# Token sums joined, gates of three batches loaded at once, and a weight quarter moved between value blocks, in a fused attention and expert-mixture kernel

## The chip, the cores and the metric

The kernel runs on one core of one Trainium2 chip. The metric is the device time of one execution in microseconds (us). A core has a tensor engine (PE, with PEld for its weight loads), a vector engine (VectorE, DVE in the profile), a scalar engine (ScalarE, ACT), GpSimd (POOL) and a queue engine (SyncE, SP). Each works through its own instructions in the order in which the program gives them, and waits on semaphores for the others. Transfers are issued by POOL (software queue) and by SP and ACT (hardware queue) and share 16 DMA engines.

## The reference, cut to what matters

Attention over 4 batches, 8 heads, 768 tokens and head size 64, in which a query sees 4 sink tokens and the last 128 tokens; its output, as 3072 rows of 512, goes through a mixture of 4 experts.

```python
keep = is_sink | ((rel >= 0) & (rel < 128))
a = softmax(where(keep, q @ k.T / 8, -1e9))
x = (a @ v).transpose(0, 2, 1, 3).reshape(3072, 512)
p = domain_probs / (domain_probs.sum(-1, keepdims=True) + 1e-09)
for e in range(4):
    out += p[:, e:e + 1] * (relu(x @ w1[e]) @ w2[e])     # w1[e]: 512x1024, w2[e]: 1024x512
```

## The kernel before, in words

**Tiling.** A batch has three groups of 256 tokens. For a group and a pair of heads, attention makes scores (`scores`, L704), exponentials on ScalarE (L729), a mask product on VectorE (L723, in batch 0 L738), and values (`values`, L763 for the sinks and L770 for the rest); reciprocals (L797) and a product (L800, or L815 on ScalarE) give `onat`, which is turned into `xT`: in batch 0 by PE (`turn`, L834, copied out at L286), later by a DMA transpose on SP (L787). In `values` the first index of `od` behind the partitions is the half of the group's 256 tokens, so `xT[b, g][:, 0]` holds the first 128 tokens and `xT[b, g][:, 1]` the second.

**The mixture.** A unit is a group and an expert. Its first product, with w1, is plain for the units that come before `START` (L1114) and else a seven-product scheme in place of eight (L1204; for the last 20 units with tokens on the partitions, L1316). The scheme needs four sums of token blocks for each group, made in `tokens` (L1170) into a tile `T`, and sums of the weight blocks: `weight_form1` (L390 to L396, tiles `vf`) and `weight_form` for w2 (L357 to L363, tiles `wf`). A unit's result, gated and clipped, lies in `H`. The second product is plain for the first two groups of batch 0 (L1575, evacuated by VectorE at L1585 and L1587 from two PSUM tiles, `acc` 0 and 1, in turn) and the seven-product scheme after that (L1489, with sums of blocks of `H` at L1430 and L1407).

**Gates.** Most units multiply by a row of gates, broadcast to all partitions by DMA (`load_gate`, L475). The 20 units with tokens on the partitions ("turning" units) use `own_gates`, which holds the probabilities by token; `own_load` (L1613) loads it, `own_made` (L1616) divides it by its sums with four VectorE operations (L1618 to L1621). `OWN = 2` says that it begins with batch 2, and `TURNED_UNITS = (4, 0)` that the turning units are all but the first four from there. A turning unit's result is made in a half-buffer (`rest`, or a resting gate tile) and brought into its `H` by a DMA transpose on SP (L1297).

**H buffers.** `NH = 6` tiles `H` in a pool, and three more in the freed `qkT` once attention is over (`widened`). A unit takes its `H` when it opens (`opened`), turning units too.

**The order of the work.** The kernel's own planner writes out the order of every engine's instructions. It keeps a clock for each engine in `t`, a cost for each kind of operation (`pe`, `act`, `dve`, `pool`, `sp`), and puts evacuations and sums into `pend` with a ready time and a slack; `flush` takes them in turn. The loop from L1660 picks the next PE step among attention, first products, second products. `idle_products` (L577, L580) writes PE products without use where the planner sees a gap in the first 20 us. `SOON` is the planner's time from which weight sums may be written while batch 0's attention is still going on (L1708); `SHARE_OF` sets how fast attention of the next batch advances beside the mixture.

**The first loads.** POOL issues two value blocks `vx`, four blocks of q and k, two more value blocks, and then the four quarters of w1 of expert 0 (L505 to L513). Between them it makes `sel2` (L522) and the batch's sink values `vsd` (L643).

Of the kernel before, what the change touches and what calls it, by code (L numbers as in the profile page):

```python
# [16 lines left out]
def kernel(  # L17
# [44 lines left out]
    OWN = 2  # L62
    TURNED_UNITS = (4, 0)
# [4 lines left out]
    SHARE_OF = (1.01, 0.92, 0.96)  # L68
# [18 lines left out]
    SCALED = 300  # L87
    SHARED = 2
# [4 lines left out]
    SOON = 34000  # L93
    NEARLY = 2
    ROWED = 24000
    GATED = 38000
    W2AT = 2
# [411 lines left out]
    load_v(0, (2, 3))  # L509
    load_w1(0, 4, [0])  # L510
    load_w1(0, 4, [1])
# [235 lines left out]
    def values(b, hp, g):  # L747
# [6 lines left out]
        for qi in range(2):  # L754
            qb = 2 * g + qi
            terms = []
            c = 0
            for (kb, q0, nq) in GROUPS[g]:
                if q0 <= qb < q0 + nq:
                    terms.append((kb, c + (qb - q0) * P))  # L760
                c += nq * P
            if g > 0:
                nc.tensor.matmul(  # L763
                    od[:, qi], lhsT=sinkA[b][:, (qb - 2) * P:(qb - 1) * P], rhs=vsd[b][:, hp],
                    start=True, stop=False, skip_group_check=True,
                )
                cols += 2 * DX
            for ph in range(2):
                for i, (kb, c) in enumerate(terms):
                    nc.tensor.matmul(  # L770
                        od[:, qi, ph], lhsT=a[:, ph, c:c + P], rhs=vx[kb][:, 2 * hp + ph, 0:DX],
                        start=(g == 0 and i == 0), stop=(i == len(terms) - 1), skip_group_check=True,
                    )
                    cols += DX + 5
# [174 lines left out]
    NH = 6  # L949
# [6 lines left out]
    class Mixture:  # L956


        def __init__(self):
# [14 lines left out]
            self.turning = set(mine[TURNED_UNITS[0]:len(mine) - TURNED_UNITS[1]])  # L974
            self.gated = [u for u in self.order if u not in self.turning]
# [9 lines left out]
            self.stored, self.homed = [], False  # L985
            self.spare, self.lent = [], {}
# [7 lines left out]
        def room(self):  # L994
            if self.units and self.units[0] in self.turning and self.halves() < 2:
                return False
            return self.spare or self.live < NH

# [13 lines left out]
        def widened(self):  # L1012

            x = sb.tile([P, 2, NHP, S], BF16, name="qkT", tag="qkT", bufs=1)
            x = x.rearrange("p i h n -> p (i h n)")
            n = 2 * QF * 2 * P
            self.spare = [x[:, i * n:(i + 1) * n].rearrange("p (k f t n) -> p k f t n", k=2, f=QF, t=2) for i in range(3)]
            self.rest("onat", 2, 2, t["pe"])
            self.rest("aT", 4, 1, t["pe"])

        def opened(self, b, g, e):

            if self.spare:
                self.H[b, g, e] = self.spare.pop()
                self.lent[b, g, e] = self.H[b, g, e]
            else:
                self.H[b, g, e] = mo.tile([P, 2, QF, 2, P], BF16, name="H", tag="H", bufs=NH)
                self.live += 1
            fast = self.is_fast(b, g, e)
            if (b, g, e) in self.turning:  # L1030
                self.G[b, g, e] = [self.half(), self.half()]

            def complete(at):
                self.H_at[b, g, e] = at
                self.finished.add((b, g, e))
                if (b, g) >= PAIRS[0]:
                    self.waiting.append((b, g, e))
                    load_gates()
                    if not TURNED_UNITS[1] and self.gated[-1] == (b, g, e):
                        self.rest_gates()  # L1040

# [19 lines left out]
        def firsts(self):  # L1061
# [15 lines left out]
            if n < WIDE and self.units and (self.units[0][0] or loaded) and early <= MIX and self.room() and not (early + zero and self.live >= NH - 1):  # L1077
                yield self.unit_ready(*self.units[0], QF), (OPEN if n else 2) - EARLY, ("unit",)
# [67 lines left out]
        def tokens(self):  # L1146
# [13 lines left out]
            B11, B21, B12, B22 = x[:, 1, 0:2], x[:, 1, 2:4], x[:, 0, 0:2], x[:, 0, 2:4]  # L1160
# [5 lines left out]
            self.T[b, g] = {"P1": B11, "P2": B21, "P3": B22, "P4": T[:, 3], "P5": T[:, 0], "P6": T[:, 1], "P7": T[:, 2]}  # L1166
            steps = [(T[:, 0], B12, B11), (T[:, 1], B22, T[:, 0]), (T[:, 2], B22, B12), (T[:, 3], B21, T[:, 1])]

            def run(engine):
                nc.vector.tensor_sub(*steps.pop(0))  # L1170
                done = dve(G, rate=1.92)
# [109 lines left out]
        def emit_turning(self, u, m, ready):  # L1281
            b, g, e = u["unit"]
            H, X, at = self.H[b, g, e], self.G[b, g, e], u["at"]
            n = QF * P
            assert len(own_steps) == 4
            if m in ("P1", "P5"):
                spare = [i for i in range(6) if ring[i] <= ready + 40]
                spare.sort(key=lambda i: (whole[i], ring[i]))
                if m == "P1":
# [5 lines left out]
                    def turned(k):  # L1295
                        def turn(at):
                            nc.sync.dma_start(  # L1297
                                out=H[:, k].rearrange("c f t n -> c (f t) n"), in_=X[k].rearrange("p f t n -> p (f t n)"), transpose=True,
                            )
                            done = sp(at, issue=1330, takes=1400, turning=True) + LANDS  # L1300
                            self.H_part[b, g, e](done)
                            self.H_part[b, g, e](done)
                            self.resting.append((done, X[k]))
# [83 lines left out]
        def chore(self):  # L1387
# [12 lines left out]
            if self.last:  # L1400
                b, g, e = u = self.last[0]
                if (b, g, "P2") not in self.products:
                    self.last.pop(0)

                    def form(engine):
                        H12 = self.H[b, g, e][:, 1, :, 0]
                        nc.vector.tensor_sub(H12, H12, self.S[b, g][1][:, e])  # L1407
                        self.S4_at[u] = dve(QF * P, rate=1.92)
                    return go(form, self.until(b, g, e, "P3"))
# [9 lines left out]
            self.waiting.pop(0)  # L1419
            if (b, g) not in self.S:  # L1420
                self.S[b, g] = [mo.tile([P, E, QF, P], BF16, name=f"S{i}", tag=f"wide{i}", bufs=1) for i in range(2)]
            H = self.H[b, g, e]
            H11, H21, H22 = H[:, 0, :, 0], H[:, 0, :, 1], H[:, 1, :, 1]
            S = self.S[b, g]
            steps = [(nc.vector.tensor_add, S[0][:, e], H21, H22), (nc.vector.tensor_sub, S[1][:, e], S[0][:, e], H11),
                     (nc.vector.tensor_sub, H21, H11, H21)]

            def form(engine):
                x = steps.pop(0)
                x[0](*x[1:])  # L1430
                at = dve(QF * P, self.stored[-1] if (b, g) == PAIRS[0] else 0.0, rate=1.92)
                if steps:
                    go(form, self.until(b, g, e, "P6 P7".split()[len(steps) == 2]))
                else:
                    self.S_at[u] = at
                    self.last.append(u)
            return go(form, self.until(b, g, e, "P6"))
# [5 lines left out]
        def operand(self, b, g, e, m):  # L1443
            H = self.H[b, g, e]
            if m in ("P5", "P6"):
                return self.S[b, g]["P5 P6".split().index(m)][:, e]
# [23 lines left out]
        def emit_product(self):  # L1470
# [30 lines left out]
            if m == CHAIN[-1]:  # L1501
                if (b, g, e) in self.lent:
                    self.spare.append(self.lent.pop((b, g, e)))
                else:
                    self.live -= 1
# [56 lines left out]
        def emit_second(self):  # L1562
# [35 lines left out]
            if s == 1:  # L1598
                self.live -= 1
# [16 lines left out]
    def own_made():  # L1616
# [13 lines left out]
        later("dve", t["pe"], 5000, run)  # L1630
# [29 lines left out]
    while mix.more() or att.more():  # L1660
# [14 lines left out]
        if rowed == 1 and now > GATED:  # L1675
            rowed = 2
            load_gates()
        if not att.more() and not loaded:
            loaded = 1
            turns += [(1, tb) for tb in range(NQB)]  # L1680
            loads.append((load_w1, 3))
            for tb in range(NQB):
                if tb == W2AT:
# [26 lines left out]
        if ahead + 1 < B and not att.more() and (ahead == 0 or (ahead + 1, 0) in turned_at) and (ahead == 0 or mix.done >= sum(work[:ahead]) * LEAD[ahead - 1]):  # L1710
            ahead += 1
            if ahead == 1:
                own_load()
            elif ahead == 2:
                own_made()
# [14 lines left out]
        opts.append((max(p, now), HIGH_PRODUCT if behind > BEHIND or mix.live >= FULL or wide and TURN_ABOUT and mix.turn_about else LOW_PRODUCT, "product", None))  # L1730
# [65 lines left out]
```

## Time and profile before

| | |
|---|---|
| median of 3 runs | 354.03 us (353.99 to 354.43) |
| the profiled execution's own time | 354.08 us |
| its span, first to last instruction | 352.4 us |
| granted PE clock | 1.00 |
| busy share PE, PEld, DVE, ACT, POOL | 98%, 76%, 81%, 59%, 21% |
| DMA | 45.61 MB, mean 129 GB/s |

All times inside the execution count from the span's start. "Busy" counts instructions that work; a matmul's end is modelled, so a busy PE need not be at its peak. A row such as `15.70 0.39 PE L580 ... x2` reads: from 15.70 us, for 0.39 us, on PE, line 580, two instructions; in brackets at its end stands idle time before it and what ended that. The chain of waits is the path back from the last instruction, at each step to what released it.

### The profile page before, as it was taken

The page shows a single profiled execution, that of the slowest core. Times are in us where ns is not written, and L with a number is a line of the kernel's source. Part 1 is how long each engine was busy: PE and PEld are TensorE (multiplying, and loading weights), DVE is VectorE, ACT ScalarE, POOL GpSimd, SP SyncE. Part 2 cuts the span into 40 slices and gives each one's busy share as a digit, 9 for nine tenths or more (in the row PEclk, how much of TensorE's full clock was granted, in tenths as well). Part 3 has the DMA queues.
Part 4 walks back from the last instruction along what each step waited for, and adds up shares of the span by engine and source line. Part 5 has one row for each costly group of instructions (what it writes and reads, how often), then busy time and mean ns, then how long its engine had stood idle before and what let it go on. Part 6 is the DMA issues. An engine that isn't in the chain of part 4 may idle for free.

```text
span 352.4 us, 9356 instructions
## 1 busy us (share of the span) xinstructions
PE 346.4 (98%) x3722; PEld 266.8 (76%) x3722; DVE 284.1 (81%) x673; ACT 207.9 (59%) x475; POOL 73.6 (21%) x91
## 2 busy tenths in 40 slices
PE   7999999999999999999999999999999999999996
PEld 3685769756789998998999886755856676666685
DVE  6886999978999999799898999578768586675740
ACT  6763723438775443647463439689579767666611
POOL 8966114340442606000152000000000000000000
PEclk9999999999999999999999999999999999999999
DMA  9999999999999999720999513646438743645541
GB/s 178 177 188 195 221 216 180 176 158 178 154 141 133 148 205 110 95 70 6 91 204 169 85 38 55 126 96 121 86 84 166 134 96 91 121 116 111 75 120 61
DMA packets 161032, 45.61 MB, mean 129 GB/s; under 512 B 144740, under 2 KB 156996, under 8 KB 160988
## 3 DMA queue, kind: packets, MB, share of 16 engines
q0 software_dynamic: 79104, 17.31, 56.0%
q1 hardware_dynamic: 80828, 27.18, 42.4%
q8 instruction: 29, 0.48, 0.6%
q10 hardware_dynamic: 1056, 0.52, 0.5%
q14 instruction: 15, 0.12, 0.1%
HBM read 38.39 MB, written 6.34 MB: 127 GB/s over the span
## 4 chain that ended last, share of the span: by engine, by line
PE 94%; DVE 3%; DMA 2%; POOL 0%; issue 0%; ACT 0%; DVEq 0%
PE acc L1489 35%; PE cps L1204 18%; PE cps L1316 17%; PE acc L1575 8%; PE hps L1114 7%; PE sps L704 3%; PE od L770 3%; DMA vx<-in_v_dram 2%; PE od L763 1%; DVE aT L738 1%; DVE T L1170 1%; DVE onat L800 1%; PE tx L834 1%; PE tr L601 0%; PE sinks L665 0%; PE acc L580 0%
## 5 line engine op out<-in xcount | busy, mean ns | idle before, releaser
L1489 PEld LDWEIGHTS <-H 128*128 128x128 bf16 x708 | 66.6, 98 | 17.8 <-issue 1.1
L729 ACT ACTIVATE aT<-sps 128x512 bf16<-128x512 f32 (+1 forms) x96 | 47.2, 579 | 16.7 <-PE sps L704 16.6
L1489 PE MATMUL acc<-w,H 128*128 128x256 bf16 x420 | 56.8, 273 | 0.0
L1204 PEld LDWEIGHTS <-w 128*128 128x128 bf16 x640 | 39.2, 98 | 1.2 <-issue 0.5
L1489 PEld LDWEIGHTS <-S 128*128 128x128 bf16 x320 | 30.4, 98 | 9.4 <-issue 0.8
L1237 DVE SCALAR_TENSOR_TENSOR H<-cps,gates 128x512 bf16<-128x512 f32 x54 | 36.4, 681 | 0.0
L1334 ACT ACTIVATE cps<-cps 128x512 f32<-128x512 f32 x44 | 25.5, 585 | 17.4 <-PE cps L1316 17.0
L1114 PE MATMUL hps<-xT,w 128*128 128x256 bf16 x256 | 31.9, 273 | 0.2 <-DVE H L1129 0.2
L815 ACT ACTIVATE onat<-od,R 128x64 bf16<-128x64 f32 x108 | 24.9, 324 | 11.4 <-DVE R L797 11.1
L315 POOL DMA_DIRECT2D vx<-in_v_dram x24 | 21.4, 898 | 45.1 <-PE od L770 34.0
L1204 PEld LDWEIGHTS <-vf 128*128 128x128 bf16 x480 | 29.3, 98 | 1.0 <-issue 0.5
L1575 PE MATMUL acc<-w,H 128*128 128x512 bf16 x128 | 29.9, 379 | 0.0
L1489 PE MATMUL acc<-wf,H 128*128 128x256 bf16 (+1 forms) x216 | 29.6, 272 | 0.0
L1114 PEld LDWEIGHTS <-w 128*128 128x128 bf16 x256 | 24.2, 98 | 4.9 <-issue 1.1
L1337 ACT ACTIVATE rest<-cps,own_gates 128x512 bf16<-128x512 f32 x37 | 25.5, 693 | 0.7
L723 DVE TENSOR_TENSOR aT<-aT,mask 128x1024 bf16<-128x1024 bf16 (+1 forms) x36 | 22.6, 637 | 3.1 <-ACT aT L729 2.9
L250 POOL DMA_DIRECT2D qkn<-in_q_dram x22 | 19.6, 893 | 25.7 <-DMA qkT<-qkn 18.1
L1204 PE MATMUL cps<-T,w 128*128 128x128 bf16 x320 | 24.3, 219 | 0.0
L1204 PE MATMUL cps<-xT,w 128*128 128x128 bf16 x320 | 24.1, 219 | 0.0
L1316 PE MATMUL cps<-w,T 128*128 128x512 bf16 x80 | 23.8, 379 | 0.0
L1316 PE MATMUL cps<-vf,T 128*128 128x512 bf16 x80 | 23.6, 379 | 0.0
L1550 ACT COPY osb<-acc 128x256 f32<-128x256 f32 x32 | 12.1, 381 | 19.3 <-PE acc L1489 19.1
(145 smaller groups left out, 676.6 us busy)
## 6 DMA issues: line engine op xcount, KB each, us to landing
w<-in_moe_w_dram POOLq DMA_DIRECT2D x6, 1024.0 KB, 18.5
out_dram<-osb SPq DMA_DIRECT2D x16, 256.0 KB
vx<-in_v_dram POOLq DMA_DIRECT2D x24, 128.0 KB, 6.7
qkn<-in_q_dram POOLq DMA_DIRECT2D x22, 128.0 KB, 6.9
qkn<-in_k_dram POOLq DMA_DIRECT2D x22, 128.0 KB, 7.1
gates<-gate_rows SPq DMA_DIRECT2D x20, 128.0 KB
w<-in_moe_w_dram POOLq DMA_DIRECT2D x4, 256.0 KB, 7.4
w<-in_moe_w_dram POOLq DMA_DIRECT2D x2, 512.0 KB, 10.8
```

The lines of the kernel that those rows point to most:

```text
L315: nc.gpsimd.dma_start(out=vx[tb][:, :, 0:D], in_=v[b, :, tb * P:(tb + 1) * P, :].rearrange("h p d -> p h d"),)
L723: nc.vector.tensor_mul(a, a, m[:, None, :].to_broadcast([P, 2, w]))
L729: nc.scalar.activation(out=a[:, ph], in_=sps[ph][:, 0:w], func=AF.Exp, scale=scale)
L815: nc.scalar.mul(o[:, qi, hp, ph * D:(ph + 1) * D], od[:, qi, ph, 0:D], R[:, qi, ph])
L1114: nc.tensor.matmul(h[:, i].rearrange("p (q n) -> p q n", q=2), lhsT=w1_sb[e][:, db, fb * P:(fb + 1) * P], rhs=xT[b, g][:, :, db], start=(i ...
L1204: nc.tensor.matmul(y[:, f], lhsT=A[:, d, f * P:(f + 1) * P], rhs=T[:, d], start=(m in ("P1", "P5") and f == 0 and d == 0), stop=(d == 1), ...
L1237: nc.vector.scalar_tensor_tensor(out=dst, in0=src, scalar=0.0, in1=gate, op0=ALU.max, op1=ALU.mult)
L1316: nc.tensor.matmul(y.rearrange("p f n -> p (f n)"), lhsT=T[:, d], rhs=A[:, d], start=(m in ("P1", "P5") and d == 0), stop=(d == 1), skip_g ...
L1334: nc.scalar.activation(out=src, in_=src, func=AF.Relu)
L1337: nc.scalar.mul(X[k][:, :, s], src, gate)
L1489: nc.tensor.matmul(y, lhsT=self.operand(b, g, e, m)[:, f], rhs=forms[e][m][:, f, cs], start=(k == 0 and f == 0 and m in (("P1", "P5", "P2" ...
L1575: nc.tensor.matmul(op, lhsT=H[:, fb // QF, fb % QF, s], rhs=w2_sb[e][:, fb, :], start=(fb == 0), stop=(fb == NFB - 1),)
```

## The change

**Joined token sums.** For batches 1 to 3 `values` now writes the halves of a group in the other order (`qi ^ (b > 0)`), so that the halves of `xT` change places. Then two of the four token sums are one operation over 512 columns. The sums are formed in another order too: two of the four now depend on none of the others, in all batches. Batch 0 keeps four operations.

**Gates by token.** `OWN = 1` and `TURNED_UNITS = (16, 0)`: `own_gates` covers three batches in place of two (18 token blocks in place of 12) and is loaded beside the second call of `load_gates` (planner's time over 38000 ns); it is divided 20000 ns of the planner's time after attention turns to batch 1, in place of when it turns to batch 2. The set of turning units stays as it was.

**First w1 quarter.** It is issued between the value blocks 2 and 3.

**H.** The six tiles are slices of one tile. A turning unit takes its slice when its result is turned, in place of when it opens (`turn_rows`); freed slices are taken in the order in which they came free.

**Planner's constants.** `SOON` goes from 34000 to 24000 and the first `SHARE_OF` from 1.01 to 1.03. New constants (`EXTRA`, `JOIN`, `ALTER`, `PROMISED`, `WAITS`) stand at values at which their branches do nothing.

```diff
-    OWN = 2
-    TURNED_UNITS = (4, 0)
+    OWN = 1
+    TURNED_UNITS = (16, 0)
-    SHARE_OF = (1.01, 0.92, 0.96)
+    SHARE_OF = (1.03, 0.92, 0.96)
-    SOON = 34000
+    SOON = 24000
...
-    load_v(0, (2, 3))
+    load_v(0, (2,))
     load_w1(0, 4, [0])
+    load_v(0, (3,))
     load_w1(0, 4, [1])
...
-                    od[:, qi], lhsT=sinkA[b][:, (qb - 2) * P:(qb - 1) * P], rhs=vsd[b][:, hp],
+                    od[:, qi ^ (b > 0)], lhsT=sinkA[b][:, (qb - 2) * P:(qb - 1) * P], rhs=vsd[b][:, hp],
...
-            B11, B21, B12, B22 = x[:, 1, 0:2], x[:, 1, 2:4], x[:, 0, 0:2], x[:, 0, 2:4]
+            one, two = (0, 1) if b else (1, 0)
+            B11, B21, B12, B22 = x[:, one, 0:2], x[:, one, 2:4], x[:, two, 0:2], x[:, two, 2:4]
...
-            steps = [(T[:, 0], B12, B11), (T[:, 1], B22, T[:, 0]), (T[:, 2], B22, B12), (T[:, 3], B21, T[:, 1])]
+            steps = [(T[:, 2], B22, T[:, 0]), (T[:, 3], B21, T[:, 2])]
+            if b:
+                steps = [(T[:, 0:2], x[:, 1].rearrange("p (i d) n -> p i d n", i=2), x[:, :, 0:2])] + steps
+            else:
+                steps = [(T[:, 0], B12, B11), (T[:, 1], B22, B12)] + steps
...
+            self.homes = [mo.tile([P, NH, 2, QF, 2, P], BF16, name="H", tag="H", bufs=1)]
+            self.spare += [(self.homes[0], i) for i in range(NH)]
...
+        def turn_rows(self, new=False):
+            late = self.unturned[:-1] if new else self.unturned[:]
+            for x in list(self.unturned):
+                u, k, at = x
+                if u not in self.H:
+                    if self.free() <= (u != self.promised[0]):
+                        continue
+                    self.promised.remove(u)
+                    self.home(u)
+                self.unturned.remove(x)
+                X = self.G[u][k]
+                nc.sync.dma_start(
+                    out=self.H[u][:, k].rearrange("c f t n -> c (f t) n"), in_=X.rearrange("p f t n -> p (f t n)"), transpose=True,
+                )
...
             load_gates()
+            if OWN == 1:
+                own_load()
...
-            if ahead == 1:
+            if ahead == 1 and OWN > 1:
                 own_load()
-            elif ahead == 2:
-                own_made()
+            elif ahead == OWN:
+                own_made(0 if OWN > 1 else 20000)
```

161 lines of the change are left out of this document (112 added, 49 removed).

## The prediction

> **What bounds the kernel now.** First the page, rows 1 and 4:
>
> ```profile
> PE 346.4 (98%) x3722; PEld 266.8 (76%) x3722; DVE 284.1 (81%) x673; ACT 207.9 (59%) x475; POOL 73.6 (21%) x91
> PE 94%; DVE 3%; DMA 2%; POOL 0%; issue 0%; ACT 0%; DVEq 0%
> ```
>
> PE holds 94% of the chain, and busy is not inflated by waits: its 3722 matmuls at their spacing in the timeline (about 56 ns for 128 columns, 109 for 256, 216 for 512) add up to 347 us of the 352.4. What a change of order can win is the rest: filler matmuls (L580), waits in the first 24 us, and a few waits later (0.14 us at 80, 0.11 at 103, 0.15 at 243 between matmul starts). So the next view is the chain of waits in the head, 13 to 30 us (start, length, what):
>
> ```profile
> 14.21 0.64 DVE T L1170
> ...
> 14.95 1.52 DVE T L1170 x3
> 16.47 1.34 DVE aT L738 x4
> 17.81 0.60 DVE H L1129
> ...
> 22.77 0.30 DVE xT L286
> ...
> 23.11 3.33 PE hps L1114 x29
> ```
>
> From 14 to 23 us VectorE sets the end, not PE: token sums, masks, an evacuation, the scaled rows. PE's timeline shows what hangs on that, and where the fillers stand:
>
> ```profile
> 15.70 0.39 PE L580 MATMUL acc<-lent 128*128 128x256 bf16 x2
> 15.93 1.04 PE L1114 MATMUL hps<-xT,w 128*128 128x256 bf16 x8
> ...
> 18.47 1.03 PE L1114 MATMUL hps<-xT,w 128*128 128x256 bf16 x8 [0.19 <-DVE H L1129]
> ...
> 26.28 5.34 PE L1575 MATMUL acc<-w,H 128*128 128x512 bf16 x24
> ```
>
> Last, VectorE by stage: the table of windows (PE, PEld, DVE, ACT, POOL busy) and its own timeline about 28 us:
>
> ```profile
> 60.00:80.00 20.00, 20.00 (x187) 13.52 (x185) 16.57 (x31) 8.89 (x18) 8.42 (x10) 1.00 1.77 167
> 100.00:120.00 20.00, 20.00 (x279) 18.20 (x277) 19.89 (x55) 11.29 (x38) 9.62 (x11) 1.00 1.77 142
> ...
> 27.75 0.18 DVE L946 TENSOR_TENSOR scale_t<-scale_t,rs 128x16 f32<-128x16 f32 x1
> 28.21 0.75 DVE L1585 TENSOR_SCALAR osbw<-acc,scale_t 128x512 f32<-128x512 f32 x1 [0.28 <-PE acc L1575]
> 29.93 0.75 DVE L1585 TENSOR_SCALAR osbw<-acc,scale_t 128x512 f32<-128x512 f32 x1 [0.97 <-PE acc L1575]
> ```
>
> Around 100 to 120 us VectorE is full as well, and PE still never waits for long.
>
> **The change part by part.** PE's matmuls, in the changed program's order, are the same but for two fillers. Order differs in four places only: 15 to 24 us, some 37 to 42, 101 to 143, 161 to 173; after that a few groups trade places.
>
> *Joined sums.* A 256-column sum starts 0.20 us after the one before it. The nearest row to a joined one is a mask product over 512 bf16 columns (L738), 0.34 apart. A group costs 0.34 + 2 x 0.20 in place of 4 x 0.20, so 0.06 us of VectorE less, 0.5 us over nine groups. Bounds: nothing saved if the overlapping read runs at the rate of a float32 operation (0.60), 1.8 saved if the joined one cost no more than a single. None of it is on the path: PE does not wait for these nine groups.
>
> *Gates by token.* L1618 to L1621 take 116.65 to 117.76 us with one other sum (0.33) between them, so 0.78, in VectorE's fullest stage. They move to about 64 to 67 us, where VectorE idles 3.4 of 20 us; with 18 blocks in place of 12 some 0.85. Nothing is queued right behind them there but weight sums, whose users come later; without that idle time they would cost the 0.85. The load keeps its place on SP (39.6 us) but grows from 1536 to 2304 packets of 16 bytes. The trace's packets of that size took 22 ns, so 768 x 22 / 16 = 1.06 us more on each DMA engine near 46 to 50 us. Behind it on the software queue are w2 of expert 2 (landed 52.4, first used by PE near 64) and w1 of expert 3 (landed 57.5, summed from 63.8): the margins of 6 us and more hide it. The next SP issue is at 56.3.
>
> *First w1 quarter.* Value blocks 2 and 3 landed at 13.49 and 14.17, the quarter at 15.34. One place earlier it lands near 13.49 + 1.17 = 14.7, and value block 3 near 15.4, needed from 17.3. PE's sinks end at 15.1, so the first L1114 starts there in place of 15.93; the fillers (0.23) go. What is late next is VectorE, whose queue from 14.1 to 22.2 has the same operations in nearly the same order. Walking it by the rows: token sums until 16.40, three masks of 0.34, then the evacuation (0.68) to 18.10; the second L1114 can start at 18.13 (0.34 earlier than before, but with one head pair's values, 0.43, left to do); the third 20.05, held by a mask; the next turn 21.04, held by scaled rows; the fourth 21.70; the first L1114 of the next group 22.69, against 22.57 before. So the freed PE time becomes wait, and the head costs +0.12. Bounds: -0.55 (below, first rival) to +0.3.
>
> *Weight sums earlier (SOON).* In the new order two sums of w1 of expert 0 (L390, L392; 0.68 each, 0.70 when one reads the other's result) stand on VectorE ahead of the first evacuation, L1585. The planner books 200 columns for L943 to L946; they took 26.89 to 27.93. So VectorE is free near 28.05, the sums take it to 29.36, and L1585 ends at 30.11. The third group of L1575 writes the same PSUM tile and would start at 29.74 + 0.12 = 29.86; it starts near 30.16: +0.30. The second evacuation ends near 31.4, ahead of its need at 32.4. Bounds: 0 (if PE is later anyway) to +2.0 (second rival). Taken out of 32 to 41 us the sums free time there, where nobody waits.
>
> *The rest.* In the full stage I summed VectorE's and PE's rows in the new order from 95.6 us: the tightest margin between a VectorE result and PE's need is -0.06 us (a mask near 99.5), before it was -0.03; near 121 us VectorE has 0.6 us to spare where before it had none. Zero there, 0.5 either way. Turned units take their slice of H later: 12 of the 40 transposes on SP wait for PE's last product with the slice, 7 before; behind them are output stores and other transposes. From a turned unit's last first-product to its second product lie at least 5.2 us of PE's rows in both orders, and a transpose holds its issue for 1.2 to 1.9: zero. Every writer of the joined H tile waits only for users of its own slice. SHARE_OF acts through the order alone.
>
> **Sum.** 0.12 + 0.30 = +0.42 on the profiled execution's 354.08 (span 352.4 and 1.7 around it, untouched), 354.5; the median lies 0.05 under that execution: 354.45, say 354.4. A measurement of this kernel tells about 0.2%, 0.7 us, from no change, so the forecast is no change, on the slow side.
>
> **Rivals.** *The token sums slip past GpSimd.* The first two sums took 0.70 and 1.12 us against 0.28 usually, and end when GpSimd's L522 and L643 end (14.71, 15.92); the second waited for the first, and L643 began in that gap. In the new order it no longer waits, so it may run at once, and L643 after it. Then the sums end near 15.6, the masks follow ScalarE's exponentials, the second L1114 needs no wait, and the next group starts near 22.02, 0.55 earlier; with the 0.30 kept: 353.8. Against it: the fourth sum still reads the third, so the same gap comes two sums later, before any mask can use the time. The Trainium skill (SBUF — State Buffer, SBUF: two separate sides) calls the port pair that VectorE and GpSimd share an exclusive lock, which goes to whichever operation starts first. By that rule the second sum wins, and this rival's time holds unless L643 gets in before the fourth; the two long rows agree with a lock.
>
> *The early weight sums meet GpSimd's transfers* (slower). Place: 28.0 to 29.4 us, where POOL issues w2 of expert 2 (27.62 to 28.50) and w1 of expert 3 (28.80 to 29.55). If they lose what the token sums lost beside L522 and L643 (0.42 to 0.84 each), the third L1575 waits 0.8 to 1.7 us longer than 0.30: 355.3 to 356.2. It decides from a delay of 0.3 us on the two together. Against it: sums and masks between 16.0 and 18.6, beside the same kind of issuing, took their usual 0.28 and 0.41.
>
> *The new order is tighter all along.* VectorE is freer from 95 us, and the head goes as planned: the fillers (0.23) and the waits at 17.9, 18.5, 21.5 and 23.1 (0.13, 0.35, 0.30, 0.22) go, and half of the 0.4 later: about 1.4 us, 352.7. For it: 0.8 us less on VectorE in its full stage. Against it: PE hardly waits there now, and the head is bound by the same VectorE work.
>
> *The joined sum is no faster.* Then nine groups lose 0.2 us each on VectorE, beside a PE that does not wait: the forecast's time.
>
> **How the numbers follow.** Forecast 0.45 (0.33 within 0.2%, 0.11 above for delays of the 101 to 143 us order, 0.01 below); slipping past GpSimd 0.10 (0.08 within, 0.02 below); early sums meet transfers 0.21, slower; tighter all along 0.24, faster. Together faster 0.27, same 0.41, slower 0.32. The range reaches into both outer rivals: 352.9 to 355.6; the forecast's own is 353.9 to 355.0.
>
> **What would show it.** Right: the first L1114 near 15.1 with two fillers fewer; the second held by L1129; L1585 ending near 30.1 and the third L1575 group waiting for it by some 0.3; no new PE waits of over 0.2 us from 95 to 175. Wrong: the group after 22 us starting before 22.3; L390 or L392 over 1 us; L1575 without a wait; a PE wait on SP's transposes.

## The result: slower by a quarter of a per cent, and the profile after

The changed kernel takes 354.92 us (median of 11 runs, 354.53 to 355.31) against 354.01 (353.84 to 354.50) of the kernel before beside it: ratio 1.0023, 95% interval 1.0015 to 1.0031. The profiled execution took 354.89 us, its span is 353.2. The medians of a_nosoon and a_nosums below include one execution each of over 362 us, in a slower state of the chip; without it they are 356.1 and 354.5. In this section and the next, lines are those of the changed kernel; L1585 of before is L1681, L1575 is L1671, L1114 is L1177, L665 is L672, L390 and L392 are L396 and L398. Rows of other kernels carry their own kernel's numbers, which differ from these or from those of before by a few lines.

Of the profile's page, the row of busy time, the sum of the DMA packets, and the chain by engine:

```profile
PE 347.3 (98%) x3720; PEld 267.1 (76%) x3720; DVE 284.8 (81%) x665; ACT 207.1 (59%) x473; POOL 73.0 (21%) x91
...
DMA packets 161799, 45.61 MB, mean 129 GB/s; under 512 B 145508, under 2 KB 157764, under 8 KB 161756
...
PE 73%; DMA 20%; POOL 4%; DVE 2%; issue 0%; ACT 0%; POOLq 0%; SPq 0%
```

Two fillers and eight VectorE operations fewer (nine token sums less and, on balance, one operation more elsewhere), 767 packets more. The chain seems to have moved from TensorE to DMA. The chain of waits from 16 to 30 us (start, length, what) shows how:

```profile
16.00 3.48 POOL qkn L256 x4
19.48 9.15 DMA vx<-in_v_dram
...
28.64 0.69 DVE vf L398
29.33 0.67 DVE osbw L1681
```

L398 names a DMA as the last to release it. VectorE's rows about 28 us tell that it cost nothing: L396 ran until 28.60, and L398, which reads its result, starts 0.72 us after L396's start, as in all nine kernels measured here that have the two one behind the other.

```profile
27.41 0.17 DVE L951 TENSOR_SCALAR rs<-rs 128x4 f32<-128x4 f32 x1
...
27.92 0.68 DVE L396 TENSOR_TENSOR vf<-w 128x1024 bf16<-128x1024 bf16 x1
28.64 0.69 DVE L398 TENSOR_TENSOR vf<-vf,w 128x1024 bf16<-128x1024 bf16 x1
29.25 0.75 DVE L1681 TENSOR_SCALAR osbw<-acc,scale_t 128x512 f32<-128x512 f32 x1
```

A chain followed through semaphores can change its engine while nothing changed in time; it has to be read beside the timeline. TensorE's timeline:

```profile
15.90 1.05 PE L1177 MATMUL hps<-xT,w 128*128 128x256 bf16 x8
...
18.53 1.03 PE L1177 MATMUL hps<-xT,w 128*128 128x256 bf16 x8
...
22.96 3.87 PE L1177 MATMUL hps<-xT,w 128*128 128x256 bf16 x32
...
26.67 5.34 PE L1671 MATMUL acc<-w,H 128*128 128x512 bf16 x24
...
87.13 0.29 PE L672 MATMUL sinks<-qkT,ksd 128*32 128x256 bf16 x4 [0.19 <-DMA qkT<-qkn]
```

The first expert group starts at 26.67 (before 26.28), and its 24 matmuls take 5.34 us as before: the foreseen wait inside it is not there. The last line is a new wait, on the DMA transposes of batch 1's queries and keys; in the kernel before the same line shows none:

```profile
86.48 0.29 PE L665 MATMUL sinks<-qkT,ksd 128*32 128x256 bf16 x4
```

The windows of 20 us (PE, PEld, DVE, ACT and POOL busy, clock, DMA share, GB/s):

```profile
60.00:80.00 20.00, 20.00 (x189) 13.71 (x187) 16.91 (x35) 8.50 (x17) 9.11 (x11) 1.00 1.83 171
...
100.00:120.00 20.00, 20.00 (x281) 18.16 (x280) 19.55 (x51) 11.74 (x39) 9.31 (x12) 1.00 1.67 139
```

VectorE's full stage lost 0.34 us of work (19.89 to 19.55) and 60 to 80 us gained as much, as the change says. TensorE hardly gained by it, as the third row of the table shows. Where the 0.82 us of the span went is read from five starts on TensorE's timeline, common to both kernels:

| TensorE reaches | before | after | lost since the row above |
|---|---|---|---|
| first expert group (L1671) | 26.28 | 26.67 | 0.39 |
| sinks of batch 1 (L672) | 86.48 | 87.13 | 0.26 |
| sinks near 140 us | 140.01 | 140.60 | -0.06 |
| sinks near 221 us | 220.35 | 221.12 | 0.18 |
| end of the span | 352.37 | 353.19 | 0.05 |

So the loss has three places: the start, the wait at 87 us, and something between 140 and 221 us. The last is a pause of VectorE, which the timeline shows without a reason (the operation waits for matmuls that ended by 179.34):

```profile
179.49 0.18 DVE L804 RECIPROCAL R<-od 128x4 f32<-128x4 f32 x1
180.03 0.69 DVE L1306 SCALAR_TENSOR_TENSOR H<-cps,gates 128x512 bf16<-128x512 f32 x1 [0.36 <-PE cps L1273]
```

TensorE loses 0.28 us behind it by 183.4, and wins 0.10 us elsewhere in that stretch.

### The profile page after: what moved, and what is told of

Read it like the earlier page. It is cut to its first block, busy times and chain, and to the rows that moved or that the text cites. A ratio compares the mean times of both kernels' runs of the same rounds, so it can differ in the third digit from the quotient of the medians.

```text
span 353.2 us, 9333 instructions
## 1 busy us (share of the span) xinstructions
PE 347.3 (98%) x3720; PEld 267.1 (76%) x3720; DVE 284.8 (81%) x665; ACT 207.1 (59%) x473; POOL 73.0 (21%) x91
## 4 chain that ended last, share of the span: by engine, by line
PE 73%; DMA 20%; POOL 4%; DVE 2%; issue 0%; ACT 0%; POOLq 0%; SPq 0%
PE acc L1586 34%; PE cps L1380 17%; PE cps L1273 14%; DMA qkn<-in_q_dram 8%; DMA qkn<-in_k_dram 6%; DMA qkT<-qkn 3%; DMA vx<-in_v_dram 3%; PE sps L711 2%; PE od L777 2%; POOL qkn L256 2%; PE hps L1177 1%; PE od L770 1%; POOL vx L321 1%; DVE H L1306 1%; PE acc L1671 0%
## 5 line engine op out<-in xcount | busy, mean ns | idle before, releaser
L1586 PEld LDWEIGHTS <-H 128*128 128x128 bf16 x732 | 68.3, 98 | 18.5 <-issue 1.4
L1586 PE MATMUL acc<-w,H 128*128 128x256 bf16 x432 | 58.7, 273 | 0.0
L1306 DVE SCALAR_TENSOR_TENSOR H<-cps,gates 128x512 bf16<-128x512 f32 x54 | 36.3, 679 | 0.5 <-PE cps L1273 0.4
L1177 PE MATMUL hps<-xT,w 128*128 128x256 bf16 x256 | 31.8, 273 | 0.1
L1586 PE MATMUL acc<-wf,H 128*128 128x256 bf16 (+1 forms) x232 | 30.6, 270 | 0.0
L1671 PE MATMUL acc<-w,H 128*128 128x512 bf16 x128 | 29.9, 379 | 0.0
L1177 PEld LDWEIGHTS <-w 128*128 128x128 bf16 x256 | 24.0, 98 | 4.9 <-issue 1.1
L730 DVE TENSOR_TENSOR aT<-aT,mask 128x1024 bf16<-128x1024 bf16 (+1 forms) x36 | 22.6, 637 | 2.2 <-ACT aT L736 2.0
L1273 PE MATMUL cps<-T,vf 128*128 128x128 bf16 x320 | 23.3, 219 | 0.0
L1380 PE MATMUL cps<-w,xT 128*128 128x512 bf16 x80 | 23.0, 379 | 0.0
```

Of the source, the lines that this page charges most:

```text
L730: nc.vector.tensor_mul(a, a, m[:, None, :].to_broadcast([P, 2, w]))
L1177: nc.tensor.matmul(h[:, i].rearrange("p (q n) -> p q n", q=2), lhsT=w1_sb[e][:, db, fb * P:(fb + 1) * P], rhs=xT[b, g][:, :, db], start=(i ...
L1273: nc.tensor.matmul(y[:, f], lhsT=A[:, d, f * P:(f + 1) * P], rhs=T[:, d], start=(m in ("P1", "P5") and f == 0 and d == 0), stop=(d == 1), ...
L1306: nc.vector.scalar_tensor_tensor(out=dst, in0=src, scalar=0.0, in1=gate, op0=ALU.max, op1=ALU.mult)
L1380: nc.tensor.matmul(y.rearrange("p f n -> p (f n)"), lhsT=T[:, d], rhs=A[:, d], start=(m in ("P1", "P5") and d == 0), stop=(d == 1), skip_g ...
L1586: nc.tensor.matmul(y, lhsT=self.operand(b, g, e, m)[:, f], rhs=forms[e][m][:, f, cs], start=(k == 0 and f == 0 and m in (("P1", "P5", "P2" ...
```

## The experiments

All of them, with the ratio to the kernel before that ran beside them. A name with a_ stands for the changed kernel with one thing altered, one with b_ for the kernel before with one thing altered. "Group" is the start of the first expert group in the profile, "GB/s" the DMA rate from 4.5 to 5.5 us, and "wait" what TensorE loses ahead of the sinks near 87 us beyond the 0.09 us that this place costs anyway (in a_nosoon, whose order differs, these sinks come at 90 us).

| kernel | us | before | ratio, 95% interval | group | GB/s | wait |
|---|---|---|---|---|---|---|
| before | 354.01 | | | 26.28 | 348 | 0 |
| after | 354.92 | 354.01 | 1.0023, 1.0015 to 1.0031 | 26.67 | 290 | 0.26 |
| a_now1 | 354.70 | 354.12 | 1.0014, 1.0005 to 1.0022 | 26.44 | 294 | 0.09 |
| a_nosoon | 356.23 | 354.12 | 1.0059, 1.0042 to 1.0076 | 26.80 | 300 | 0 |
| a_noown | 354.41 | 354.12 | 1.0007, 0.9999 to 1.0016 | 26.10 | 348 | 0.13 |
| a_nosums | 354.55 | 354.12 | 1.0007, 0.9998 to 1.0016 | 26.52 | 297 | 0.21 |
| b_w1soon | 354.45 | 354.17 | 1.0009, 1.0000 to 1.0017 | 26.41 | 346 | 0 |
| b_sums | 354.18 | 354.17 | 1.0002, 0.9993 to 1.0010 | 26.16 | 349 | 0 |
| a_onlyown | 354.56 | 354.17 | 1.0014, 1.0005 to 1.0023 | 26.81 | 291 | 0 |
| b_soon | 354.42 | 354.17 | 1.0006, 0.9997 to 1.0015 | 26.48 | 348 | 0 |
| b_pad | 354.52 | 354.08 | 1.0012, 1.0003 to 1.0021 | 26.62 | 294 | 0 |
| a_aligned | 354.85 | 354.08 | 1.0020, 1.0010 to 1.0029 | 26.38 | 347 | 0.82 |
| a_shift | 354.91 | 354.08 | 1.0022, 1.0013 to 1.0031 | 26.65 | 307 | 0.17 |
| a_short | 354.69 | 354.04 | 1.0018, 1.0009 to 1.0027 | 26.39 | 347 | 0 |

**First: one part undone at a time.** In a_now1 the quarter goes back behind the value blocks:

```
-    load_v(0, (2,))
+    load_v(0, (2, 3))
     load_w1(0, 4, [0])
-    load_v(0, (3,))
```

> The changed kernel with one part undone: the first w1 quarter is loaded behind both value blocks again, as before. The two traces differ by 0.39 us where the first group behind the token sums starts on TensorE (22.96 us against 22.57). Theory A: this reordering makes that 0.39 us; then the group starts near 22.6 us again and the time falls from 354.92 to about 354.5 us. Theory B: the 0.39 us is made ahead of it, at the start (the first key cast on ScalarE began at 4.97 us against 4.62, and TensorE's first transposes ran late behind it), by nothing that was edited; then the group starts between 22.5 and 23.0 us as the first cast starts early or late, and the time stays at 354.7 to 355.1 us.

Measured: 354.70 us, 0.22 less than the changed kernel; the first expert group starts at 26.44, the first key cast at 4.88. The group behind the token sums starts at 22.74 where theory A had 22.6, and the median falls on the edge of B's range. The start scatters, but what moves it is not shown yet.

```
-    SOON = 24000
+    SOON = 34000
```

> The changed kernel with SOON back at 34000, so that the sums of the w1 halves L396 and L398 are issued behind the first two expert group evacuations again and the order of attention and expert work up to 162 us changes with them. The prediction's term: third expert group of 26 to 31 us waits 0.30 us in the changed kernel; its trace shows no such wait (24 expert matmuls in 5.34 us, as before). Theory A (early sums cost 0.30 us somewhere): 354.6 us. Theory B (they cost nothing in the head, but the order they bring makes the wait of 0.35 us at 87.13 us): the wait there goes and the time is about 354.65 us. Theory C (neither): 354.9 us, with the wait at 87 us still there.

All three theories missed: 356.23 us, 1.3 more. With the quarter moved and SOON at 34000 the order from 28 to 162 us is another one, and in it TensorE takes 46.41 us from the sinks at 95 to those near 141, 1.25 more than in the kernel before. Its waits there, and VectorE's line ahead of the second:

```profile
102.45 0.61 PE L1273 MATMUL cps<-T,vf 128*128 128x128 bf16 x8 [0.34 <-ACT aT L736]
...
115.20 0.61 PE L1273 MATMUL cps<-T,w 128*128 128x128 bf16 x8 [0.58 <-DVE cps L1326]
```

```profile
113.19 0.42 DVE L1239 TENSOR_TENSOR T<-xT 128x512 bf16<-128x512 bf16 x1 [0.56 <-DMA xT<-onat]
```

A joined sum waits 0.56 us for the transposed xT, the evacuations L1306 and L1326 are queued behind it, and TensorE waits for L1326. So SOON at 24000 is no edit of its own: without it the planner writes another order around the other parts. Which of them brings this about was not tried.

```
-    OWN = 1
-    TURNED_UNITS = (16, 0)
+    OWN = 2
+    TURNED_UNITS = (4, 0)
```

> The changed kernel with the gates by token made for two batches again (1536 packets of 16 B and no 768 more) and loaded later, and the units of batch 1 no longer turned on the SP queue in that number (OWN 2, TURNED_UNITS (4, 0)). Theory A: the DMA transpose of batch 1's queries and keys that TensorE waits for at 87.13 us (0.35 us) is late through this load or the transposes beside it; then that wait goes and the time is about 354.65 us. Theory B: the moved gates work costs nothing; then 354.9 us. Theory C (it saves what the prediction put on it, nothing, but its order hides something now): 355.1 us or more.

354.41 us, 0.5 less: more than theory A's 0.27. The wait at 87 us shrinks to 0.13 and stays; VectorE's pause near 180 us is gone; and the group starts at 26.10, although no engine's order differs from the changed kernel's up to the load at 39 us.

For a_nosums the four sums, the pairs of P6 and P7 and the order of the value products are those of before:

```
-            steps = [(T[:, 2], B22, T[:, 0]), (T[:, 3], B21, T[:, 2])]
-            if b: ...
+            steps = [(T[:, 0], B12, B11), (T[:, 1], B22, T[:, 0]), (T[:, 2], B22, B12), (T[:, 3], B21, T[:, 1])]
```

> The changed kernel with the four token sums of a group one by one and in the old order and places again (eight VectorE instructions more in all), the halves of the value products in the old order. Theory A: the joined sums are worth their 0.06 us a group only off the critical path, and the old order of the first batch's sums is the better or the worse by nothing: 354.9 us. Theory B: the joined sums move the VectorE order behind 175 us, and the wait of 0.21 us at 183.36 us goes with them: about 354.65 us. Theory C: the separate sums meet GpSimd's selection of 14.9 to 16.0 us with two of four sums as before and the head is 0.1 to 0.4 us later: 355.0 to 355.3 us.

354.55 us, 0.37 less, and no pause near 180 us: theory B by its sign.

**Second: one part alone in the kernel before.** b_soon sets SOON to 24000; b_w1soon has this and the moved quarter; b_sums has the reordered and joined sums; a_onlyown is the changed kernel with everything but the gates of three batches undone.

> The kernel before with SOON at 24000 alone: the two weight sums ahead of the first expert group's evacuation, nothing else moved behind 38 us. Theory A (the prediction's term: the third expert group waits 0.30 us on TensorE near 30 us): 354.4 us, and the wait is in the trace at 30 us. Theory B (VectorE reaches the sums late enough that they run in the gap ahead of the evacuation, as in the changed kernel's trace): 354.1 us and no wait.

> The kernel before with two parts of the change alone: the first w1 quarter between the value blocks and SOON at 24000. Behind 38 us its order on every engine is that of the kernel before, so it shows the head by itself. Theory A (the prediction's sum): 0.12 us of the head and 0.30 us of the earlier weight sums are lost, 354.1 becomes 354.5 us. Theory B (the 0.39 us by which the changed kernel's profile was late at 26 us was the start's own scatter: the profiles so far reach the first expert group L1671 between 26.10 and 26.80 us with the same order ahead of it): the time stays at 354.0 to 354.2 us. Theory C (two fillers of 0.11 us fewer come through to the end): 353.9 us. The wait of TensorE at 87 us is not in theory B unless the slack there is under 0.1 us.

354.42 and 354.45 us, 0.25 and 0.28 more than before; both intervals reach down to no change, so the traces have to carry the reading. TensorE's and VectorE's timelines of b_w1soon, with GpSimd's beside them:

```profile
26.41 5.62 PE L1576 MATMUL acc<-w,H 128*128 128x512 bf16 x24
```

```profile
27.21 0.47 DVE L945 TENSOR_SCALAR rs<-rs 128x4 f32<-128x4 f32 x1
...
28.02 0.68 DVE L390 TENSOR_TENSOR vf<-w 128x1024 bf16<-128x1024 bf16 x1
28.74 0.69 DVE L392 TENSOR_TENSOR vf<-vf,w 128x1024 bf16<-128x1024 bf16 x1
29.35 0.74 DVE L1586 TENSOR_SCALAR osbw<-acc,scale_t 128x512 f32<-128x512 f32 x1
```

```profile
26.95 0.75 POOL L328 DMA_DIRECT2D w<-in_moe_w_dram  x1
```

The 24 matmuls take 0.28 us longer; the gap lies ahead of the third group of L1576, which starts at 30.15 when the evacuation has ended at 29.35 + 0.74 = 30.09. In b_soon it is 0.21. That is theory A in both; the prediction had 30.16 for this start and 0.30 for the wait. The new reading is the first of VectorE's lines: an operation on 4 elements that takes 0.47 us here, 0.42 in the kernel before, and 0.17 in the changed kernel. It ends with GpSimd's DMA issue (27.21 + 0.47 = 27.68, and 26.95 + 0.75 = 27.70). Without these 0.30 us the evacuation would end at 29.79, before the third group can start (26.41 + 16 x 0.216 = 29.87), and there would be no wait.

> The kernel before with the reordered and joined token sums alone (8 VectorE instructions fewer). Taking them out of the changed kernel gained about 0.37 us and took away the VectorE pause ahead of 183 us. Theory A (that pause needs the moved gates too, since taking those out also removes it): the time stays at 354.0 to 354.2 us. Theory B (the joined sums alone bring it): about 354.4 us. Theory C (the 0.06 us a group on VectorE comes through where VectorE is the bound, 95 to 122 us): 353.9 us or less.

354.18 us: theory A. The joined sums cost nothing and gain nothing by themselves.

> The changed kernel with only the gates of three batches and what goes with them left (OWN 1, 16 units turned, the new bookkeeping of the blocks); w1 order, SOON, SHARE_OF and token sums are as before. Taking this part out of the changed kernel gained 0.5 us. Theory A (it costs 0.5 us by itself): 354.6 us. Theory B (it costs through the VectorE pause near 183 us, which needs the joined sums, and through the wait at 87 us, which needs the new head): 354.1 to 354.2 us.

354.56 us: theory A by the median, though it had named no place. From the first group on its profile is 0.08 us faster than that of before (326.01 us against 326.09 to the end). All of the loss lies ahead of 26.81 us, where no engine's order differs. What differs is the DMA rate at 4.5 us, and with it, in every profile so far, whether the kernel has the gates of three batches. These are 96 B longer for each partition, own_sum is longer as well, and every tile allocated behind them lies 128 B higher: kraw at 196224 B, no multiple of 512 any more, instead of 196096.

**Third: the address by itself.**

```
-    own_sum = consts.tile([P, OWNED], FP32, name="own_sum")
+    own_sum = consts.tile([P, OWNED + 32], FP32, name="own_sum")[:, 0:OWNED]
```

> The kernel before with nothing changed but an address: the tile own_sum is 128 B longer per partition, so that every tile allocated behind it lies 128 B higher, as the larger own_gates and own_sum make it in the changed kernel (kraw at 196224 B instead of 196096, which is a multiple of 512). In the five profiles with that shift the DMA engines moved 286 to 307 GB/s between 4.5 and 5.5 us, while the first queries and keys land in elements of 512 B; in the five without it 344 to 349. Theory A (the shift of the addresses is what the moved gates cost: a_onlyown lost 0.39 us with no wait added behind 27 us): 354.15 becomes about 354.5 us, the rate at 4.5 to 5.5 us falls to about 295 GB/s, and the first key cast on ScalarE begins at 4.9 us. Theory B (the rate has another cause, or the start's loss is made up): 354.1 to 354.2 us.

Theory A to 0.02 us: 354.52. The windows of before, of after, and of b_pad (the last two columns are DMA share and GB/s):

```profile
4.50:5.50 1.00, 1.00 (x12) 0.72 (x11) 0.56 (x4) 0.62 (x1) 1.00 (x3) 1.00 1.15 348
```

```profile
4.50:5.50 1.00, 1.00 (x5) 0.39 (x4) 0.47 (x3) 0.53 (x1) 1.00 (x3) 1.00 1.20 290
```

```profile
4.50:5.50 1.00, 0.91 (x8) 0.57 (x6) 0.51 (x4) 0.59 (x1) 1.00 (x3) 1.00 1.20 294
```

The DMA engines are as busy, but move a sixth less; the first key cast starts at 4.91 instead of 4.62, the first expert group at 26.62 instead of 26.28. The same program, 128 B higher, loses 0.34 us at 26 us and keeps it to the end. A single start scatters by about as much (26.10 to 26.48 in the seven profiles with the addresses of before, 26.44 to 26.81 in the seven with the higher ones), but the averages, 26.31 and 26.64, lie 0.33 apart, and the first key cast starts at 4.62 to 4.79 in the former and at 4.88 to 4.97 in the latter, without overlap.

a_aligned takes the 128 B back in the changed kernel:

```
-    own_sum = consts.tile([P, OWNED], FP32, name="own_sum")
+    own_sum = vsf[:, 0, 0:OWNED]
-    held = consts.tile([P, 2], BF16, name="held")
-    half = consts.tile([P, 2], BF16, name="half")
+    both = consts.tile([P, 4], BF16, name="half")
+    half, held = both[:, 0:2], both[:, 2:4]
```

> The changed kernel with the same instructions on TensorE, ScalarE and SyncE and the addresses of the kernel before: own_sum lies in a row of vsf that is free by then, and held shares half's tile, which takes back the 128 B by which the changed kernel moved every tile behind them. Theory A (the shift costs about 0.39 us): 354.9 becomes about 354.5 us, with 345 GB/s at 4.5 to 5.5 us. Theory B (it does not): 354.9 us. The VectorE pause near 180 us (0.36 us) should stay if it hangs on the instruction stream and go if it hangs on addresses; without it another 0.2 to 0.28 us are gained.

The rate (347 GB/s) and the group (26.38) are theory A's, the time is theory B's: 354.85. What was won by 26 us is lost again at 87:

```profile
87.55 0.29 PE L672 MATMUL sinks<-qkT,ksd 128*32 128x256 bf16 x4 [0.75 <-DMA qkT<-qkn]
```

This profile is of an execution at 355.24, 0.39 above the median, and one thing in it is in no other: the transpose that SyncE issues at 75.09 holds it for 2.38 us, where the same one takes 1.24 or 1.25 in the other thirteen profiles, and the next one, for which TensorE waits, goes out at 77.58 instead of between 75.42 and 76.49. So the usual wait is probably smaller, and this profile alone cannot tell what makes it. The pause of VectorE is gone here too, though no instruction count of VectorE changed.

```
     nc.vector.memset(half, 0.0)
+    nc.vector.memset(half, 0.0)
```

> The changed kernel with one VectorE instruction more: the memset of half (0.06 us near 4.2 us, where VectorE waits for the first queries) is issued twice. Ahead of the unexplained pause of VectorE at 179.67 us (0.36 us, 0.28 us of it lost on TensorE by 183.4 us) the kernel without moved gates, which lacks the pause, has the same operations and one wait more in VectorE's stream. Theory A (the pause hangs on where the instruction lies in VectorE's stream): it goes or moves, and the time is about 354.65 us. Theory B (it hangs on the data, the order or the addresses): it stays, 354.9 us. In either case it is a second profile of the changed kernel's order: the first expert group comes between 26.1 and 26.8 us.

Theory A by the trace, theory B by the time. The pause is gone:

```profile
179.38 0.17 DVE L805 RECIPROCAL R<-od 128x4 f32<-128x4 f32 x1
179.57 0.69 DVE L1307 SCALAR_TENSOR_TENSOR H<-cps,gates 128x512 bf16<-128x512 f32 x1
```

and TensorE needs 80.24 us from the sinks near 140 to those near 221, where the changed kernel's profile has 80.52 and that of before 80.34. But the median stays at 354.91 (the profiled execution took 354.72). So the pause is seen in the profiles of after and a_now1, and not in those of a_noown, a_nosums, a_aligned, a_shift and a_short; that the timed runs pay for it is not shown, and its cause stays open.

a_short, last, goes on from a_aligned:

```
+    nc.vector.memset(own_gates[:, OWNED - 2 * NG:], 1.0)
-        nc.sync.dma_start(out=own_gates, in_=moe_domain_probs[OWN * S:]...
+        nc.sync.dma_start(out=own_gates[:, 0:OWNED - 2 * NG], in_=moe_domain_probs[OWN * S:(B - 1) * S]...
```

> The changed kernel at the addresses of the kernel before (as a_aligned), and of the gates by token only those of batches 1 and 2 are loaded: 1536 packets of 16 B as in the kernel before, not 2304. The gates of batch 3 are set to one instead, so that this part of the output is left out. a_aligned gained 0.29 us at 26 us and lost 0.92 us at 87 us, where TensorE waits for the transposed queries and keys of batch 1; its loads of these land late (its second at 75.03 us, before at 73.81). Theory A (the 768 packets more, about 1 us on each DMA engine while all 16 are busy, push the loads behind them back, and the wait at 87 us is that): the key load lands near 74 us, the wait at 87 us is 0.1 us or less, and 354.85 becomes about 354.4 us. Theory B (the wait hangs on how the queues share the DMA engines, not on these packets): 354.85 us with a wait of 0.1 to 0.9 us there.

Mixed. The wait is gone in the profile, as theory A has it; TensorE's line at that place:

```profile
86.69 0.29 PE L672 MATMUL sinks<-qkT,ksd 128*32 128x256 bf16 x4
```

Its load covers two of the three batches and so has as many packets as before; the last batch's gates are set to 1. But the first key load landed at 74.64, not near 74, and the median, 354.69, gained 0.16 of the 0.45 expected. Medians of the kernel before alone lie between 354.01 and 354.17, so a gain of 0.16 is hardly one. In its profile 0.38 of the 0.45 us over that of before come behind the start of the last matmul (3.77 us there, 3.39 to 3.64 in the other profiles); whether that is usual was not tried. SyncE's issue at 74.70 takes 1.25 us here, so the two profiles differ in more than the packets, and theory A is not shown by them.

No part and no combination that was run is faster than the kernel before.

## Why the prediction was right, and where it was not

The forecast was 354.4 us with a range of 352.9 to 355.6; it came out at 354.92, inside. The likeliest class, no change within 0.2%, missed narrowly: 0.23%, on the slow side that the forecast leaned to. The sum was 0.42 us for a change of 0.91, and its terms were not those that were paid; that the time still lies inside the range is in part luck.

- *First quarter, +0.12.* Its steps are sound, its size is too small to be seen. Among the seven kernels with the addresses of before, the group starts on average at 26.31 with the old order (26.28, 26.16, 26.48) and at 26.32 with the new one (26.41, 26.10, 26.38, 26.39), in starts that scatter by 0.3. The first L1177 comes at 15.16 to 15.28 in a_noown, a_aligned and a_short (15.59 in b_w1soon), and the second one is held by L1192 (in the changed kernel L1192 ends at 18.48, L1177 starts at 18.53). In the changed kernel itself the first L1177 is at 15.90, since everything there is late from 5 us on.
- *Weight sums, +0.30.* Right where it can be seen by itself: forecast end of the evacuation 30.11 and third group 30.16, measured 30.09 and 30.15 in b_w1soon; in a_aligned and a_short the third group waits 0.15 and 0.11 us. In the changed kernel it is zero, by the lower bound that the prediction gave (TensorE is later anyway, by 0.39 us) and because L951 missed GpSimd's issue and took 0.17. So "L1575 without a wait", listed as a sign against, came true for a reason beside the mechanism, and the 0.30 was not paid.
- *Joined sums, hidden.* Hidden they are: b_sums is the kernel before to 0.01 us. The 0.34 holds in five of the nine groups, where another operation comes next (96.22 and 96.55, 113.34 and 113.68). In the other four the next sum follows at once and reads the joined one's result: it starts 0.45 us behind it. Where all three stand together the last one starts 0.32 later, 0.78 in all, where the kernel before had 0.73 from its first to its fourth (157.00, 157.46 and 157.78, against 156.53 to 157.26). There nothing is saved. The bound "nothing saved" at 0.60 is a slip as well: 0.60 + 2 x 0.20 is 0.20 more than 4 x 0.20, as the last rival has it.
- *Gates by token, hidden.* This is the step that failed. Its compute is hidden, as said. But the tile's size was costed as time on the DMA engines and not as an address: 128 B on all tiles behind it cost 0.34 us at the start (b_pad, +0.44 in the medians). "The margins of 6 us and more hide it" looked at the two weight loads next behind on the software queue; further back stand the queries and keys of batch 1. The 768 packets do push these back. a_onlyown and b_pad have the same addresses, the first with the packets: the second value block issued behind the load lands at 63.89 against 63.26 us, the first key block at 74.61 against 74.02. There it costs nothing that can be seen: the transposes that the sinks need land at 86.59 and 86.70, TensorE waits in neither, and the medians lie 0.39 and 0.44 us over those of the kernel before beside them.
- *The wait at 87 us.* "A PE wait on SP's transposes" was among the signs of being wrong, and it is there. What makes it stays open. It is seen in six of the seven profiles with the changed kernel's order there (0.09 to 0.82 us; 0 in a_short), among them a_noown, which has the short load, and in none of the six with the order of before. No part that was undone takes it away for certain, and SHARE_OF was not tried by itself.
- *The two do not add up.* The moved gates cost 0.39 us by themselves (a_onlyown), by b_pad all of it the address as far as such medians tell, and 0.51 in the changed kernel (a_noown against it). Yet a_aligned, which has the moved gates at the addresses of before, is no faster than the changed kernel: in its profile the early start is lost again at 87 us. Whether its other executions lose it there as well is not shown.
- *The rest, 0 with 0.5 either way.* It holds: -0.06 us from 87 to 140 us, and 0.10 won between 140 and 221 but for the pause. There is no new wait of over 0.2 us from 95 to 175, as said. a_nosoon shows that the order of the full stage can cost a microsecond.

The rivals. *Slipping past GpSimd*: in a_noown the second sum does run at once, and then the next one meets L650, as the argument against it said; in the changed kernel it is the first, as VectorE's timeline shows:

```profile
15.09 1.06 DVE L1239 TENSOR_TENSOR T<-xT 128x256 bf16<-128x256 bf16 x1
...
16.07 0.28 DVE L1239 TENSOR_TENSOR T<-xT 128x256 bf16<-128x256 bf16 x1
```

In each of the fourteen profiles one of the four sums takes 1.06 to 1.22 us, whichever is there. *Early sums meet GpSimd's transfers* had the sign and nearly the size (355.3), but not the mechanism: L396 and L398 took 0.68 to 0.69 us in every profile, well under the 1 us named. *Tighter all along*: VectorE has 0.34 us less to do from 100 to 120 us, not 0.8, and TensorE gained 0.06 us between 87 and 140.

## What to carry to other kernels

A tile that grows moves every tile behind it: where a change touches a size, compare addresses before orders, and if they moved, measure the kernel before with a pad of that size. The margin of a load has to be looked for at every transfer behind it that shares the DMA engines, not at the next one alone: here loads that landed 5 and 16 us after the last of its packets still came 0.6 us late. Where two late things can meet at one place, undoing either may show nothing, so a part that wins nothing when it is undone is not yet free.

## What the hardware showed that was not expected

- *512 B elements at an offset of 128 B.* Over 4.5 to 5.5 us, seven profiles with kraw and qraw at multiples of 512 B moved 346 to 349 GB/s, seven with them 128 B higher 290 to 307. A packet of 512 B took 27.0 ns on average there in each of the former, 31.8 to 33.5 in the latter. That it is the address is shown (b_pad); which mechanism is not. The Trainium skill (DMA: Bandwidth & Descriptors, How a descriptor splits into AXI transactions) says that transactions start at multiples of 256 B, so that an unaligned start costs beats; by it 512 B from an offset of 128 take 20 beats instead of 16, an estimate of 278 GB/s for 348. The trace agrees in direction and is 4 to 10% above that; the Trainium skill speaks there of what is read, and here the written side moved.
- *A tiny VectorE operation can wait for GpSimd's DMA issue.* The 4-element TENSOR_SCALAR behind the reduction (L945 and its like) took 0.17 us in seven profiles. In the other seven, that of before among them, it took 0.28 to 0.47: there it began 0.26 to 0.46 us after the start of a 0.75 us issue (L328, L334) and ended 0.01 to 0.03 us before the issue did. Begun 0.03, 0.07, 0.07 and 0.16 us after an issue's start, it took 0.17; in the other three of the quick seven no such issue was under way, or the one under way had at most 0.13 us left. The Trainium skill (SBUF — State Buffer, SBUF: two separate sides) has the shared port pair locked for the whole of an instruction. The slow seven agree with a lock; the four that began early in an issue agree only if the issue takes the lock some way in.
- *The spacing of TensorE's first matmuls.* The first 13 fillers took 3.85 us before and 4.83 after, with the granted clock at 1.00 in every window (TensorE's timeline of before, then of after):

```profile
1.40 3.85 PE L580 MATMUL acc<-lent 128*128 128x512 bf16 x13 [1.40 <-DVE lent L486]
```

```profile
1.40 4.83 PE L587 MATMUL acc<-lent 128*128 128x512 bf16 x13 [1.40 <-DVE lent L492]
```

  Those of 512 columns start 0.427 us apart until, between 4.0 and 7.3 us in the fourteen profiles, the spacing for a given width halves. It looks like the cause of the late start and does not explain it: b_w1soon (4.87 us) has its first group at 26.41, b_pad (3.90) at 26.62. Among the seven kernels with the higher addresses it may add to it: the first group comes at 26.44 to 26.62 where the 13 fillers took 4.41 us or less, and at 26.65 to 26.81 where they took 4.83 or more.
